# Regrouping the small matrix products of a delta-rule attention step that is woven into a feed-forward block

## The chip, the cores and the metric

The kernel runs on one core of one Trainium2 chip. The metric is the device time of one execution in microseconds (us), smaller is better. A core has five engines with a queue each: TensorE (PE in the profile; PEld are its weight loads), VectorE (DVE), ScalarE (ACT), GpSimd (POOL) and SyncE (SP, which issues transfers). They run side by side and wait for one another through semaphores; each takes its own instructions in the order of its queue. Products land in PSUM, which has eight banks of 512 fp32 columns on 128 partitions.

## The reference

A delta-rule attention over 4 x 8 heads of 768 tokens with 48 dimensions each, and after it a feed-forward block with a PReLU:

```python
# q, k, v: (4, 8, 768, 48); beta: (4, 8, 768)
k_n = k / (norm(k, axis=-1) + 1e-6)
state = zeros(B, H, D, D)
for t in range(S):
    y[:, :, t] = q[t] @ state
    v_old      = state.T @ k_n[t]
    state      = state + beta[t] * outer(k_n[t], v[t] - v_old)
x = y.transpose(0, 2, 1, 3).reshape(3072, 384)
h = x @ w_in                                      # (3072, 2048)
g = maximum(h, 0) + alpha * minimum(h, 0)
return g @ w_out                                  # (3072, 384)
```

All in fp32.

## The kernel before

The sequence is cut into 12 chunks of 64 tokens. A *step* n is one chunk of one pair of batches, 16 heads; there are 24 steps, and steps alternate between the two pairs, so step n continues the state of step n - 2. Inside a chunk the recurrence is a triangular system. Its 32 x 32 diagonal blocks are inverted on VectorE for four steps at once (`eliminate(m)`, where group m holds steps 4m to 4m + 3); the rest is small products on TensorE, 16 of them for each name below, in quarters of the array (64 x 64):

- `grams(n)`: k times k, the system's entries; made several steps ahead, as `eliminate` needs four steps of them
- `flips`: transposes of k and q through the identity, with copies by ScalarE
- `placing(n)`: ScalarE puts the inverted blocks where the products want them (`diag`, `inv`)
- `between_1(n)`, `between_2(n)`: the block of the inverse off the diagonal, in two products with a copy between them
- `through_state(n)`: what the old state gives to the values, the scores and the output (two products)
- `solve(n)`: the inverse times the right-hand side, giving `u`
- `outputs(n)`, `next_state(n)`: scores times `u` for the output, k times `u` for the state
- `to_ffn(n)`: transposes of the output for the feed-forward block

The feed-forward block of an earlier chunk is a generator of pieces: `ffn_in` (48 pieces a chunk, each a 128 x 128 by 256 product) and `ffn_out_fast` (28 pieces of two products of 192 columns; seven products of half matrices in place of eight). After each pair of `ffn_in` columns ScalarE and VectorE apply the PReLU. `weave` interleaves generators by shares. From step 4 on:

```python
def attention(n):
    place(n + 1, (0,))
    through_state(n)
    between_1(n + 1)
    yield
    solve(n)
    grams(n + EARLY)            # EARLY = 8
    between_2(n + 1)
    scale_v(n + 1)
    yield
    outputs(n)
    next_state(n)
    load_late(n + 2)
    squares(n + EARLY + 1)
    yield
    flips(n + EARLY + 1, n + 2)
    to_ffn(n)
    weigh(n + EARLY + 1)        # square root on ScalarE, reciprocal on VectorE
    load_early(...); load_q(n + 3); load_v(n + 3)
    yield

for n in range(NJ, N):          # NJ = 4, N = 24
    gens = [(attention(n), 4), (placing(n + 1, (1, 2, 3)), 24)]
    if n % NJ == 0 and n < N - NJ:
        m = n // NJ + 1
        blocks, left = eliminate(m), WHOLE + (PIECES if m > 2 else 0)   # 39, later 43 pieces
        share = -(-left // 3)
    if n % NJ < 3 and n < N - NJ:
        gens.append((part(blocks, share), share))
    if n < NJ + 2:
        gens.append((part(late, 12), 12))          # second product of chunk 1
    else:
        parts = IN_PARTS - 4 if n % 2 == 0 else FAST_PARTS + 4     # 44 or 32
        gens.append((part(tail, parts), parts))
    # ... weight_sums in steps 5 to 7
    weave(*gens)
```

One product with its reader, as each of them was written:

```python
def solve(n):
    p = ps_big()[:, :, 0 : G * D].rearrange("p a (g d) -> p a g d", a=2, g=G)   # own tile, two banks
    for g, a, t in quarters():                                                  # 16 products
        nc.tensor.matmul(p[half(t ^ a), a, g], inv[n % NE][half(t), a * G + g], rhs_[n][half(t), a, g])
    us[n] = work.tile([128, 2, G, D], FP32, name="u")
    nc.vector.tensor_tensor(out=us[n], in0=p, in1=..., op=ALU.mult)
```

`ps_big` hands out three tiles of two banks in turn; two single banks serve the feed-forward block.

Of the kernel before, what the change touches and what calls it, by code (L numbers as in the profile page):

```python
# [41 lines left out]
def kernel(  # L42
# [50 lines left out]
    NXT = 2  # L93

# [223 lines left out]
    def prep(n):  # L318

        if n >= N:  # L320
            return
        squares(n)
        weigh(n)
# [10 lines left out]
    def weigh(n):  # L334
        if n >= N:
            return
        c, bp = steps[n]
        norm = stats[n]
        nc.scalar.sqrt(norm, norm)
        nc.scalar.activation(norm, norm, ACT.Copy, bias=1e-6)  # L340
        rec = work.tile([128, H], FP32, name="rec")
        nc.vector.reciprocal(rec, norm)
        wgt = work.tile([128, 3, G], FP32, name="wgt", bufs=EARLY + 3)
        nc.gpsimd.tensor_tensor(out=beta_t[:, c, bp], in0=beta_t[:, c, bp], in1=rec, op=ALU.mult)
        nc.gpsimd.tensor_tensor(
            out=wgt[:, 0:2],
            in0=beta_t[:, c, bp].rearrange("p (g a) -> p a g", a=2),
            in1=rec.rearrange("p (g a) -> p a g", a=2),
            op=ALU.mult,
        )  # L350
        stats[n] = (norm, wgt)

    def flip(src, p):
        for g in range(G):
            nc.tensor.transpose(  # L355
                p[:, g * 128 : (g + 1) * 128],
                src[:, 2 * g : 2 * g + 2].rearrange("p h d -> p (h d)"),
                ident,
            )

    def flips(n_k, n_q):

        both = n_k < N and n_q < N
        p = ps_big() if both else None
        copies = []
        if n_k < N:
            p_k = p[:, 0] if both else ps_one()
            flip(early(n_k), p_k)
            k_t[n_k] = work.tile([128, G, 128], FP32, name="k_t", bufs=EARLY + 1)
            copies.append((k_t[n_k], p_k))  # L370
        if n_q < N:
            p_q = p[:, 1] if both else ps_one()
            flip(q_pad[n_q % NQ], p_q)
            q_t[n_q] = beside[steps[n_q][1]][:, :, :, D : D + C]
        for dst, src in copies:
            nc.scalar.copy(dst.rearrange("p g i -> p (g i)"), src)  # L376
        if n_q < N:
            nc.scalar.copy(  # L378
                q_t[n_q].rearrange("p t g i -> p g t i"),
                p_q.rearrange("p (g t i) -> p g t i", g=G, t=2),  # L380
            )
# [4 lines left out]
    def grams(n):  # L386

        if n >= N:
            return
        p = ps_big()[:, :, 0 : G * C].rearrange("p a (g i) -> p a g i", g=G)  # L390
        for g, a, t in quarters():
            nc.tensor.matmul(  # L392
                p[half(t), a, g], k_t[n][dims(a), g, half(t)], k_t[n][dims(a), g, half(t)]
            )
        w = stats[n][1][:, 0:2, :, None].to_broadcast([128, 2, G, HB])
        for dst, cols in (
            (gather(n), slice(0, HB)), (right[n % EARLY][:, 1:], slice(HB, C))
        ):
            nc.vector.tensor_tensor(  # L399
                out=dst.rearrange("p (a g) i -> p a g i", a=2), in0=p[:, :, :, cols], in1=w,  # L400
                op=ALU.mult,
            )
        keep(n)
# [231 lines left out]
    def between_1(n):  # L635

        if n >= N:
            return
        p = ps_big()[:, :, 0 : G * HB].rearrange("p a (g i) -> p a g i", a=2, g=G)
        for g, a, t in quarters():  # L640
            nc.tensor.matmul(  # L641
                p[half(t ^ a if changes(n) else t), a, g],
                right[n % EARLY][half(t), a * G + g : a * G + g + 2].rearrange("p b i -> p (b i)"),
                diag[n % NE][half(t), a * G + g, 0:HB],
            )
        nc.scalar.copy(
            mid[n % 2].rearrange("p (a g) i -> p a g i", a=2)[:, :, :, 0:HB], p
        )

    def between_2(n):  # L650
        if n >= N:
            return
        p = ps_big()[:, :, 0 : G * HB].rearrange("p a (g i) -> p a g i", a=2, g=G)
# [8 lines left out]
        nc.vector.tensor_tensor(out=to, in0=to if changes(n) else own, in1=p, op=ALU.add)  # L662
# [12 lines left out]
    def through_state(n):  # L675
        c, bp = steps[n]
        if c == 0:
            rhs_[n] = by_parity(nv[n])
            return
        p = ps_big()[:, :, 0 : G * (D + C)].rearrange("p a (g e) -> p a g e", g=G)  # L680
# [4 lines left out]
        p_y = ps_big()[:, :, 0 : G * D].rearrange("p a (g d) -> p a g d", g=G)  # L685
# [7 lines left out]
        for to, own, a in (  # L693
            (slice(0, 128), slice(0, 128), 0), (half(0), half(1), 1), (half(1), half(0), 1)
        ):
            nc.vector.tensor_tensor(  # L696
                out=r[to, a], in0=v_in[to, a], in1=p[own, a, :, 0:D], op=ALU.subtract
            )
        masked(n, p[:, :, :, D : D + C])
        y = work.tile([128, H, D], FP32, name="y")  # L700
        nc.scalar.copy(by_parity(y), p_y)  # L701
        rhs_[n], ys[n] = r, y

    def solve(n):
        p = ps_big()[:, :, 0 : G * D].rearrange("p a (g d) -> p a g d", a=2, g=G)
# [5 lines left out]
        nc.vector.tensor_tensor(  # L711
            out=us[n], in0=p,
            in1=stats[n][1][:, 0:3:2, :, None].to_broadcast([128, 2, G, D]), op=ALU.mult,
        )

    def outputs(n):
        c, bp = steps[n]
        p = ps_big()[:, :, 0 : G * D].rearrange("p a (g d) -> p a g d", a=2, g=G)
# [4 lines left out]
        if c == 0:  # L723
            ys[n] = work.tile([128, H, D], FP32, name="y")
            nc.scalar.copy(by_parity(ys[n]), p)
        else:
            nc.vector.tensor_tensor(
                out=by_parity(ys[n]), in0=by_parity(ys[n]), in1=p, op=ALU.add
            )

    def next_state(n):
        c, bp = steps[n]
        if c < NCH - 1:
            p = ps_big()[:, :, 0 : G * D].rearrange("p t (g d) -> p t g d", g=G)
# [5 lines left out]
            for a in range(2):  # L740
                x = state[bp][dims(a)]
                nc.vector.tensor_tensor(out=x, in0=x, in1=p[dims(a)], op=ALU.subtract)

# [219 lines left out]
    def weave(*gens):  # L963

        live = [[0.0, i, 1.0 / n, g] for i, (g, n) in enumerate(gens)]
# [9 lines left out]
    SHARES = 4  # L975

    def attention(n):


        place(n + 1, (0,))  # L980
        through_state(n)
        between_1(n + 1)
        yield
        solve(n)
        grams(n + EARLY)
        between_2(n + 1)
        scale_v(n + 1)
        yield
        outputs(n)
        next_state(n)  # L990
        load_late(n + 2)
        squares(n + EARLY + 1)
        yield
        flips(n + EARLY + 1, n + 2)
        to_ffn(n)
        weigh(n + EARLY + 1)
        load_early(n + EARLY + 1 + NKE)
        load_q(n + 3)
        load_v(n + 3)
        yield  # L1000
# [3 lines left out]
    def busy(n, p=None):  # L1004

        p = ps_one() if p is None else p
        while n > 0:
            x = p[:, 0 : int(512 * min(n, 1))]
            nc.tensor.matmul(  # L1009
                x, ident, k_t[NJ - 1].rearrange("p g i -> p (g i)")[:, 0 : x.shape[-1]]  # L1010
# [3 lines left out]
    def pair(n):  # L1014

        both = (n, n + 1)
        for i in both:
            through_state(i)
        yield
        for i in both:  # L1020
            solve(i)
            yield
        for i in both:
            outputs(i)
            next_state(i)
# [9 lines left out]
    def ready(n):  # L1035
# [7 lines left out]
        for i in both:  # L1043
            between_1(i)
# [5 lines left out]
        for i in both:  # L1050
            between_2(i)
# [23 lines left out]
    def first_chunk(mask, convert):  # L1075
# [20 lines left out]
        for i in both:  # L1096
            place(i, (1,), True)
            between_1(i)
        busy(0.5, ps_ffn())
        for i in both:  # L1100
            place(i, (2,))
            between_2(i)
        for i in both:
            through_state(i)
            solve(i)
        busy(0.5, ps_ffn())
        outputs(0)
        convert(4)
        next_state(0)
        outputs(1)  # L1110
        next_state(1)
# [9 lines left out]
    def statics(first, last):  # L1121
        if first > 0:
            squares(first)
        for n in range(first, last + 1):
            if n < last:
                squares(n + 1)
            weigh(n)
# [4 lines left out]
            if n > first:  # L1132
                grams(n - 1)
            yield
        grams(last)
# [102 lines left out]
    def prelude(n):  # L1238
        place(n)
        yield  # L1240
        between_1(n)
        yield
        between_2(n)
        yield
        scale_v(n)
        yield

    def catch_up():
        for n in range(FIRST + NJ, EARLY + NJ):
            grams(n)  # L1250
# [3 lines left out]
            weigh(n + 1)  # L1254
            load_early(n + 1 + NKE)
            yield

    late = ffn_out(1)
    few = OUT_PARTS // 4
    weave((prelude(NJ), 4), (catch_up(), 2 * (EARLY - FIRST)), (part(late, few), few))  # L1260
# [6 lines left out]
    tail = feed_forward()  # L1267
    for n in range(NJ, N):

        gens = [(attention(n), SHARES), (placing(n + 1, (1, 2, 3)), SHARES * PLACING)]  # L1270

        if n % NJ == 0 and n < N - NJ:
            m = n // NJ + 1
            blocks, left = eliminate(m), WHOLE + (PIECES if m > 2 else 0)
            share = -(-left // 3)
        if n % NJ < 3 and n < N - NJ:
            gens.append((part(blocks, share), share))
        if n < NJ + 2:
            gens.append((part(late, (OUT_PARTS - few) // 2), (OUT_PARTS - few) // 2))
        else:  # L1280
            parts = IN_PARTS - 4 if n % 2 == 0 else FAST_PARTS + 4
            gens.append((part(tail, parts), parts))
        if n == NJ + 1:
            gens.append((weight_sums(0, 0, 3), 3))
        elif n == NJ + 2:
            gens.append((chain(weight_sums(1, 0, 3), weight_sums(0, 3, 4)), 4))
        elif n == NJ + 3:
            gens.append((weight_sums(1, 3, 4), 1))
        weave(*gens)
# [32 lines left out]
```

## Time and profile before

| | |
|---|---|
| time, median of 3 (lowest to highest) | 685.09 us (684.9 to 686.08) |
| span of the profiled execution | 683.6 us |
| TensorE busy, products | 660.0 us, 9359 |
| VectorE busy, instructions | 471.3 us, 1162 |
| ScalarE busy, instructions | 249.4 us, 586 |
| HBM read and written | 31.56 and 4.72 MB |

How to read it: a product of fp32 operands appears as more than one record of TensorE (two for a large or small product, one for a transpose), and the records overlap, as products are pipelined. So the time a product costs is read from the distance between starts, not from the length of a record. `64*48 64x48` after a group's name is the part of the array (rows*columns) and the shape of the result. The number after "L" is the line of the kernel. "[1.70 <-DVE prod L477]" says that the engine stood idle for 1.70 us and what ended it. Lines to know: L840 is `ffn_in`, L904 `ffn_out_fast`, L882 the plain second product of the first chunks, L355 the flips, L751 `to_ffn`, L392 `grams`, L641 and L656 `between_1` and `between_2`, L682 and L687 `through_state`, L707 `solve`, L720 `outputs`, L736 `next_state`; on VectorE L477 and L483 are the elimination, L852 the PReLU, L711 the multiply that makes `u`.

### The profile page before, as it was taken

What the parts mean: (1) busy time and instruction counts of PE and PEld (TensorE: products, weight loads), DVE (VectorE), ACT (ScalarE), POOL (GpSimd) and SP (SyncE); (2) the same over time, 40 slices, a digit from 0 to 9 for tenths busy, and PEclk for the clock granted to TensorE, in tenths of its full rate; (3) what the DMA queues carried; (4) which work ended last, traced back from release to release, by engine and by line L of the source; (5) the groups of instructions that cost most, each with busy time, mean ns of one, the idle gap of its engine ahead of it and who ended that gap; (6) DMA issues with size and microseconds to landing.
All of it is one profiled execution on the core that took longest, in us unless ns stands there. A gap on an engine that the chain in (4) does not pass through costs nothing.

```text
span 683.6 us, 21618 instructions
## 1 busy us (share of the span) xinstructions
PE 660.0 (97%) x9359; PEld 570.2 (83%) x9359; DVE 471.3 (69%) x1162; ACT 249.4 (36%) x586; POOL 27.8 (4%) x95
## 2 busy tenths in 40 slices
PE   5989999999889999999999999999999999999997
PEld 4567777666678988988988988988989989989997
DVE  4966789879998379978479978379877255345261
ACT  4836756344434234235235235134034133231110
POOL 5000121000000000000000000000000000000000
PEclk9999999999999999999999999999999999999999
DMA  8847644211402112112112202201201211100000
GB/s 126 236 116 218 166 106 117 70 36 37 83 18 43 34 40 48 34 39 47 35 40 36 36 25 36 37 25 36 47 18 33 53 24 20 36 1 2 23 1 24
DMA packets 110958, 37.68 MB, mean 55 GB/s; under 512 B 104160, under 2 KB 107248, under 8 KB 110864
## 3 DMA queue, kind: packets, MB, share of 16 engines
q1 hardware_dynamic: 109088, 35.81, 24.0%
q8 instruction: 74, 1.21, 0.7%
q10 hardware_dynamic: 1776, 0.49, 0.4%
q14 instruction: 20, 0.16, 0.1%
HBM read 31.56 MB, written 4.72 MB: 53 GB/s over the span
## 4 chain that ended last, share of the span: by engine, by line
PE 79%; DVE 13%; ACT 3%; issue 1%; DMA 1%; SPq 1%; POOL 0%; ACTq 0%; DVEq 0%
PE p_ffn L840 32%; PE p_ffn L904 27%; PE p_big L355 3%; DVE block L483 2%; DVE prod L477 2%; PE p_big L682 2%; PE p_big L720 2%; PE p_big L707 2%; PE p_big L641 2%; PE p_big L1009 2%; DVE act L852 1%; PE p_big L656 1%; PE p_big L392 1%; PE p_big L687 1%; DMA ke<-in_k_dram 1%
## 5 line engine op out<-in xcount | busy, mean ns | idle before, releaser
L840 PE MATMUL p_ffn<-xt,w_in 128*128 128x256 f32 x1152 | 268.8, 385 | 6.2 <-DVE act L852 2.4
L840 PEld LDWEIGHTS p_ffn<-xt,w_in 128*128 128x128 f32 x1152 | 211.9, 190 | 37.0 <-issue 4.0
L852 DVE SCALAR_TENSOR_TENSOR act<-act,al_t,p_ffn 128x256 f32<-128x256 f32 x176 | 76.3, 475 | 56.8 <-ACT act L850 55.8
L850 ACT ACTIVATE act<-p_ffn 128x512 f32<-128x512 f32 x88 | 52.4, 596 | 129.7 <-PE p_ffn L840 120.1
L904 PE MATMUL p_ffn<-w_out,act 128*128 128x192 f32 x480 | 84.2, 329 | 0.3 <-DVE act L852 0.3
L904 PEld LDWEIGHTS p_ffn<-w_out,act 128*128 128x128 f32 x480 | 78.5, 190 | 1.9 <-DVE act L852 0.9
L483 DVE TENSOR_TENSOR block<-block,prod 128x30 f32<-128x30 f32 (+9 forms) x150 | 49.8, 332 | 5.2
L477 DVE TENSOR_TENSOR prod<-block 128x30 f32<-128x30 f32 (+9 forms) x150 | 48.9, 326 | 2.0
L924 DVE TENSOR_TENSOR o_sb<-u,p_ffn 128x192 f32<-128x192 f32 x40 | 13.2, 352 | 41.4 <-PE p_ffn L904 35.1
L378 ACT COPY beside<-p_big 128x512 f32<-128x512 f32 x24 | 14.0, 589 | 54.2 <-PE p_big L355 54.2
L376 ACT COPY k_t<-p_big 128x512 f32<-128x512 f32 x24 | 13.9, 580 | 51.6 <-PE p_big L355 51.5
L701 ACT COPY y<-p_big 128x384 f32<-128x384 f32 x22 | 10.5, 478 | 57.3 <-PE p_big L687 57.3
L904 PE MATMUL p_ffn<-space_out,sums 128*128 128x192 f32 x160 | 29.3, 326 | 0.0
L904 PE MATMUL p_ffn<-more,sums 128*128 128x192 f32 x160 | 29.3, 326 | 0.0
L696 DVE TENSOR_TENSOR r<-v_raw,p_big 64x192 f32<-64x192 f32 (+1 forms) x66 | 23.2, 352 | 7.3 <-PE p_big L682 6.2
L904 PE MATMUL p_ffn<-w_out,sums 128*128 128x192 f32 x160 | 27.7, 326 | 0.0
L904 PEld LDWEIGHTS p_ffn<-space_out,sums 128*128 128x128 f32 x160 | 26.6, 190 | 0.0
L904 PEld LDWEIGHTS p_ffn<-more,sums 128*128 128x128 f32 x160 | 26.6, 190 | 0.0
L441 ACT COPY same<-right 32x256 f32<-32x256 f32 x29 | 11.7, 402 | 40.1 <-DVE right L399 39.9
L904 PEld LDWEIGHTS p_ffn<-w_out,sums 128*128 128x128 f32 x160 | 25.8, 190 | 0.0
L924 DVE TENSOR_TENSOR u<-u,p_ffn 128x192 f32<-128x192 f32 x20 | 7.1, 354 | 26.4 <-PE p_ffn L904 26.3
L609 ACT ACTIVATE diag<-inverse,which 64x128 f32<-64x128 f32 (+2 forms) x60 | 24.2, 405 | 2.2 <-DVE inverse L453 1.3
(156 smaller groups left out, 948.5 us busy)
## 6 DMA issues: line engine op xcount, KB each, us to landing
w_out<-in_moe_w_in_dram SPq DMA_DIRECT2D x12, 512.0 KB, 5.0
qp<-in_q_dram SPq DMA_DIRECT2D x48, 96.0 KB, 2.9
v_raw<-in_v_dram SPq DMA_DIRECT2D x48, 96.0 KB, 2.9
kl<-in_k_dram SPq DMA_DIRECT2D x96, 48.0 KB, 2.4
out_dram<-o_sb SPq DMA_DIRECT2D x92, 48.0 KB, 1.6
space_out<-in_moe_w_out_dram SPq DMA_DIRECT2D x11, 384.0 KB, 4.3
ke<-in_k_dram SPq DMA_DIRECT2D x43, 96.0 KB, 3.1
w_out<-in_moe_w_out_dram SPq DMA_DIRECT2D x5, 384.0 KB, 3.6
```

Source lines behind the costliest of these rows:

```text
L355: nc.tensor.transpose(p[:, g * 128 : (g + 1) * 128], src[:, 2 * g : 2 * g + 2].rearrange("p h d -> p (h d)"), ident,)
L376: nc.scalar.copy(dst.rearrange("p g i -> p (g i)"), src)
L378: nc.scalar.copy(q_t[n_q].rearrange("p t g i -> p g t i"), p_q.rearrange("p (g t i) -> p g t i", g=G, t=2),)
L477: nc.vector.tensor_tensor(out=prod, in0=r[:, 0:j, j : j + 1].to_broadcast([128, j, n]), in1=r[:, j : j + 1, j + 1 : HB].to_broadcast([128, ...
L483: nc.vector.tensor_tensor(out=r[:, 0:j, j + 1 : HB], in0=r[:, 0:j, j + 1 : HB], in1=prod, op=ALU.add)
L609: nc.scalar.mul(out, x, which[rows, i : i + 1])
L696: nc.vector.tensor_tensor(out=r[to, a], in0=v_in[to, a], in1=p[own, a, :, 0:D], op=ALU.subtract)
L840: nc.tensor.matmul(p_h[:, i], w_in[:, t, (f + i) * 128 : (f + i + 1) * 128], xt[:, t], start=(t == 0), stop=(t == KT - 1),)
L850: nc.scalar.activation(g, p_h, ACT.Relu, scale=-1.0)
L852: nc.vector.scalar_tensor_tensor(out=g[:, i], in0=g[:, i], scalar=al_t[:, f + i : f + i + 1], in1=p_h[:, i], op0=ALU.mult, op1=ALU.add,)
L904: nc.tensor.matmul(p, x(i), w(i), start=(i == 0), stop=(i == FP - 1))
L924: nc.vector.tensor_tensor(out=to, in0=x, in1=p, op=ALU.add)
```

## The change

Each step has two bursts of small products instead of three. Burst A holds `outputs` and `next_state` of step n - 1 and `through_state` of step n; burst B holds `solve(n)`, `between_2(n + 1)`, `between_1(n + 2)` and `grams(n + 9)`. The products of a burst are issued back to back; products whose results fit together share one PSUM tile, and what reads them is issued after the burst (functions return the readers as a list, which `now` runs). `weigh` is split, so that the reciprocal comes later in VectorE's queue than the square root in ScalarE's. The Gram matrices are made one step earlier, the elimination of a group runs over four steps, and the feed-forward pieces come in fixed stretches between the bursts. The flips write and copy 112 rows of their result instead of 128 (two heads of 48, the second from row 64). Its purpose is to change less often between large and small products.

```diff
+    ROWS = C + D                                   # 112
 def flip(src, p):
         nc.tensor.transpose(
-            p[:, g * 128 : (g + 1) * 128],
-            src[:, 2 * g : 2 * g + 2].rearrange("p h d -> p (h d)"),
+            p[0:ROWS, g * 128 : (g + 1) * 128],
+            src[:, 2 * g : 2 * g + 2].rearrange("p h d -> p (h d)")[:, 0:ROWS],
             ident,
         )
 ...
-    def solve(n):
-        p = ps_big()[:, :, 0 : G * D].rearrange("p a (g d) -> p a g d", a=2, g=G)
+    def solve(n, p=None):
+        p = region(p, G * D, g=G)
 ...
-        nc.vector.tensor_tensor(
+        return [lambda: nc.vector.tensor_tensor(
             out=us[n], in0=p, ...
-        )
+        )]
 ...                                 # the same for the other products
-    def attention(n):               # (above)
+    def burst_a(n):
+        b = ps_big()
+        soon, later = [], []
+        if n > NJ:
+            soon += outputs(n - 1, b[:, :, 0:WY])
+            soon += next_state(n - 1, b[:, :, WY : 2 * WY])
+            later.append(lambda: load_late(n + 1))
+        if n < N:
+            p, y = ps_big(), ps_big()
+            soon += through_state(n, p[:, :, 0 : G * (D + C)], y[:, :, 0:WY])
+            if n + 1 == LATE:       # 8
+                soon += between_1(LATE, b[:, :, 2 * WY : 2 * WY + G * HB])
+            later.append(lambda: load_v(n + 3))
+        now(soon)
+        return later
+
+    def burst_b(n):
+        b, x = ps_big(), ps_big()[:, :, 0 : G * C]
+        soon = solve(n, b[:, :, 0:WY])
+        soon += between_2(n + 1, b[:, :, WY : WY + G * HB])
+        if n + 2 != LATE:
+            soon += between_1(n + 2, b[:, :, 2 * WY : 2 * WY + G * HB])
+        gram = grams(n + EARLY + 1, x)
+        now(soon + gram[:2])
+        return gram[2:] + [lambda: squares(n + EARLY + 2)]
+
+    def turn_round(n):
+        if n > NJ:
+            to_ffn(n - 1)
+        flips(n + EARLY + 1, n + 2)
+        later = weigh(n + EARLY + 1)
+        load_early(n + EARLY + 1 + NKE)
+        load_q(n + 3)
+        return later
 ...
 def prelude(n):                     # n = 4
     place(n)
+    place(n + 1, (0,))
     yield
     between_1(n)
+    between_1(n + 1)
     yield
     between_2(n)
-    yield
     scale_v(n)
     yield
+    place(n + 1, (1, 2, 3))
+    yield
 ...                                 # catch_up: one more grams and squares
+    def stretch(n, blocks, share, later, *gens):    # n feed-forward pieces, woven with
+        ...                                         # elimination (from 0.3 of it on) and `later` (from 0.5)
+    SHARES = {NJ + 2: (5, 6, 8), NJ + 3: (4, 4, 7)}                 # pieces of the elimination
+    TURNS = [(3, 3, 4), (3, 3, 4), (4, 4, 4), (3, 4, 4)]
+    FILL = {NJ: (4, 3, 3), NJ + 1: (3, 3, 2), NJ + 2: (2, 16, 12)}  # feed-forward pieces
+    FILLS = [(12, 16, 12), (12, 12, 12)]
 for n in range(NJ, N):
+    later = burst_a(n)
+    stretch(fill[0], blocks, share[0], later, *extra[0])
+    later = turn_round(n)
+    stretch(fill[1], blocks, share[1], later, *extra[1])
+    ...                             # every fourth step: place(n + 2, (0,)), next group
+    later = burst_b(n)
+    ...
+    stretch(fill[2], blocks, share[2], later + scales, *after, *extra[2])
+    ...                             # after step 6: group 2 must be done, group 3 begins
+stretch(12, iter(()), 0, burst_a(N))
+to_ffn(N - 1)
 for _ in tail:
     pass
```

## The prediction

> **What bounds the kernel now.** I read, in this order, the busy totals, the slices of the span, the chain of work that ended last, the TensorE timeline of one steady stretch, and the stretches by attention step. Totals, clock and chain:
>
> ```profile
> PE 660.0 (97%) x9359; PEld 570.2 (83%) x9359; DVE 471.3 (69%) x1162; ACT 249.4 (36%) x586; POOL 27.8 (4%) x95
> PEclk9999999999999999999999999999999999999999
> PE 79%; DVE 13%; ACT 3%; issue 1%; DMA 1%; SPq 1%; POOL 0%; ACTq 0%; DVEq 0%
> ```
>
> TensorE is the bound, at full clock, so a gain can only come from products that TensorE does faster or from waits it no longer has. The number of products isn't changed. So I look at what a change of product size costs. The timeline of TensorE in a steady step (columns: start us, length us, then the group):
>
> ```profile
> 396.96 5.02 PE L840 MATMUL p_ffn<-xt,w_in 128*128 128x256 f32 x22
> 401.90 0.68 PE L707 MATMUL p_big<-r,inv 64*64 64x48 f32 x32
> 402.40 0.66 PE L392 MATMUL p_big<-k_t 48*64 48x64 f32 x32
> 402.88 0.62 PE L656 MATMUL p_big<-diag,mid 64*64 64x32 f32 x32
> 403.43 5.45 PE L840 MATMUL p_ffn<-xt,w_in 128*128 128x256 f32 x24
> 408.81 0.68 PE L720 MATMUL p_big<-u,a_t 64*64 64x48 f32 x32
> 409.31 0.54 PE L736 MATMUL p_big<-u,kl 64*48 64x48 f32 x32
> 409.78 5.02 PE L840 MATMUL p_ffn<-xt,w_in 128*128 128x256 f32 x22
> 414.64 0.60 PE L355 MATMUL p_big<-ident,ke 128*128 128x128 f32 x4
> ...
> 640.79 20.88 PE L840 MATMUL p_ffn<-xt,w_in 128*128 128x256 f32 x96
> 661.51 5.36 PE L904 MATMUL p_ffn<-w_out,act 128*128 128x192 f32 x32
> ```
>
> The reader is to see the starts. Undisturbed, 96 records of the first feed-forward product take 661.51 - 640.79 = 20.72 us, 0.216 each. The 24 records between two bursts take 408.81 - 403.43 = 5.38, where 24 x 0.216 = 5.18 would do: 0.20 lost at the run's two ends. The burst of three small products takes 403.43 - 401.90 = 1.53 us. Single starts show groups of four records every 58 ns, eight groups a product, so 3 x 0.464 = 1.39: another 0.14 lost. Together **0.34 us a burst**. The burst of two gives the same: 0.97 us, against 0.464 + 8 x 0.045 = 0.82 (L736 steps at 45 ns), and the 0.20 beside it. Transposes (L355) follow the large products at full rate.
>
> Then the stretches by attention step, steps 4 to 8 (columns: window and length, then busy us of PE, PEld, DVE, ACT, POOL):
>
> ```profile
> 154.28:169.27 14.99, 14.09 (x293) 9.77 (x292) 14.08 (x40) 7.88 (x22) 0.45 (x3) 1.00 0.16 31
> 169.27:185.62 16.35, 14.37 (x292) 9.77 (x291) 15.59 (x38) 6.55 (x18) 0.51 (x2) 1.00 0.40 77
> 185.62:214.64 29.02, 26.08 (x357) 21.51 (x356) 25.83 (x63) 11.55 (x27) 1.57 (x4) 1.00 0.25 48
> 214.64:240.76 26.12, 26.12 (x392) 25.09 (x393) 14.11 (x31) 7.62 (x20) 0.41 (x2) 1.00 0.18 33
> 240.76:266.50 25.74, 25.74 (x384) 22.37 (x387) 21.30 (x55) 10.78 (x25) 0.41 (x2) 1.00 0.23 47
> ```
>
> From step 7 TensorE has no gap. In steps 4 to 6 (60.36 us) VectorE is busy 55.50 and TensorE stops now and then, for instance here:
>
> ```profile
> 199.26 2.40 PE L840 MATMUL p_ffn<-xt,w_in 128*128 128x256 f32 x10 [1.70 <-DVE prod L477]
> 206.41 1.97 PE L840 MATMUL p_ffn<-xt,w_in 128*128 128x256 f32 x8 [0.55 <-DVE act L852]
> ```
>
> There VectorE sets the pace, and a step's length is its queue of work.
>
> **What the Trainium skill says.** The page "TensorEngine Tiling (Array Packing)", section "Key Properties", says that changing the tiling mode, not just the tile, drains TensorE. The trace agrees: of the 0.34 us above, single starts put about a third on the way from 128*128 to 64*64 and the rest on the way back, while going from 64*64 to 48*64 (L707 to L392) costs nothing to speak of. The page "PSUM — Partial Sum Buffer", section "PSUM bank collisions raise a hardware error", wants readers and TensorE kept apart by bank, not address. In the new kernel several products of a burst share one pair of banks, so the first reader waits for the last writer of that tile; before, each product had its own tile, and no trace here shows the sharing yet. "Perfetto Trace Analysis", section "Optimization Strategy", says that a kernel can have regimes with different most-contended engines; steps 4 to 6 against the rest are such a case.
>
> **The change part by part.**
>
> 1. *Two bursts instead of three.* Before, a step has through_state + between_1, solve + grams + between_2, and outputs + next_state. After, outputs and next_state of step n-1 stand ahead of through_state of step n, and between_1 joins solve, between_2 and grams. The products are the same: 3 + 3 + 2 a step become 4 + 4. Steps 4 to 23 had 20 x 3 = 60 bursts; now there are 20 of each kind and one last for the outputs of step 23, 41. Of the 19 saved, 15 lie from step 8 on (48 become 33), where TensorE is the bound: 15 x 0.34 = **5.1 us saved**. The four of steps 4 to 7, 1.4 us, count only if TensorE sets the pace there.
>
> 2. *The flips write 112 rows instead of 128.* The transposes stream the same 128 columns of the identity; they start every 0.109 us now (L355: 0.43 for four) and will then. Copies have as many elements per partition. Zero.
>
> 3. *Dependencies.* State products of step n use the state of batch pair n mod 2, which the outputs burst before has updated; next_state(n-1) writes the other one. So nothing inside a burst waits for VectorE. From solve to outputs there are 12 feed-forward pieces, 12 x 0.432 = 5.2 us, for one VectorE multiply of 0.55 us (L711) behind the end of the burst. From through_state to solve there are 28 or 24. That is ample if VectorE's queue is short. Bursts now stand at multiples of six pieces, where one pair of feed-forward columns ends; the old cut left a wait of 0.17 us on the activation each second chunk of 51 us. Some new wait of that size may come where VectorE's queue is long after a burst: I put it at +0.5 us net.
>
> 4. *The elimination is spread over four steps instead of three.* In steps 8 and on this lowers the peaks of VectorE and is worth nothing, as TensorE doesn't wait there. In the early regime it costs: group 2 must still end with step 6, and 15 pieces of group 3 now come in step 7: four transposes of 0.61, a mask of 1.22 and ten pairs of 0.35 to 0.75, some 9.5 us. VectorE in steps 4 to 7 had 55.50 + 14.11 = 69.6 us; less feed-forward work there (16 pieces fewer) takes off some 1.4. So 69.6 + 9.5 - 1.4 = 77.7 us.
>
> 5. *Feed-forward pieces moved.* Steps 4 to 7 held 24 late output pieces and 44 + 32 = 76 of the tail; now 24 and 24 + 36 = 60. The 16 missing pieces are of the second product, 0.65 us each, 10.4 us that come later. Steps 4 to 7 took 240.76 - 154.28 = 86.5 us, so they break even at 76.1. VectorE's work is 77.7, but some 5 us of it stand in the queue behind what the burst of step 8 needs. So the burst can start at about 73, or 75 with 2 us of idle (before, VectorE idled 4.9 in steps 4 to 6). That is **0 to 3 us saved; I take 1**, in which the 1.4 of point 1 is included.
>
> 6. *The prelude* places the left part of step 5 earlier and does two between_1 in one burst; before, TensorE waited 0.9 us for a scaled copy of ScalarE ahead of the second. It also does one more Gram product, which a later step is spared. **0.5 saved.**
>
> Sum: -5.1 + 0.5 - 1 - 0.5 = -6.1. The median of 685.1 gives 679.0; I take 679.5, as point 5 rests on a queue with no gaps.
>
> **The rivals.** *Rival A: VectorE takes over.* In steps 4 to 7 its work is 77.7 us against 76.1 at break-even; with the old idle of 5 us the steps end some 6 us late and eat the gain: 684 to 686. For it: 55.50 busy of 60.36, and point 4. Against it: the pieces are woven in by shares, the square root is taken well ahead of its reciprocal, and idle of VectorE came mainly from such waits. *Rival B: new waits in each step.* If outputs wait for the solve's multiply behind other work, or the shared banks hold up a burst, at 0.3 us a step that is 6 us: again about 685. Against it: 5.2 us of slack and VectorE busy 70 to 90% of a step. *Rival C: the switch isn't the cost*, and a longer burst loses as much as two: then only points 5 and 6 remain, 683. Against it: 0.34 is the same for bursts of two products and of three.
>
> **Range and chances.** All rivals right together end near 688, all parts at their best (6.4 for the switches, 3 for early steps, 1 for the prelude) near 674.5. I put 80% on 675 to 684.5. Faster by over 2% needs 671.4, which no part offers: 0.03. Slower by over 2% needs 698.8, a new wait of a microsecond in each step: 0.02.
>
> **What would show it.** Right: TensorE's timeline has two bursts a step, a chunk of two steps shorter by 2 x 0.34 us (51.2 to 50.5 around 340 to 440 us), idle still near zero from step 8 on, and the burst of step 8 beginning at 226 to 231 us instead of 240.76, with 16 pieces more left to do. Wrong: TensorE idle in steady steps with VectorE named (u, act or y); the solve burst of four products taking clearly more than 4 x 0.464 + 0.14 = 2.0 us; VectorE busy through steps 4 to 7 with the burst of step 8 later than 232.

## The result, and the profile after

| | before | after |
|---|---|---|
| time, median of 4 (lowest to highest) | 685.59 us (684.9 to 687.79) | 691.84 us (689.12 to 692.29) |
| span of the profiled execution | 683.6 us | 690.4 us |
| start of `through_state` of step 4, then of step 8 | 154.28, 240.69 | 156.24, 239.89 |
| from `through_state` of step 8 to the end | 442.89 | 450.49 |

The kernel became slower: ratio 1.0084, interval 1.0057 to 1.011. The predicted 679.5 us and its range missed it; even the sign was wrong. Totals, clock and chain of the profile after:

```profile
PE 660.5 (96%) x9359; PEld 573.0 (83%) x9359; DVE 467.9 (68%) x1162; ACT 250.1 (36%) x585; POOL 28.2 (4%) x95
PEclk9999999999999999999999999999999999999999
PE 77%; DVE 13%; ACT 5%; SPq 2%; issue 2%; DMA 1%; POOL 0%; ACTq 0%
```

On this page the two kernels look alike, which is the first lesson: a change of 6.8 us in 690 has to be looked for in stretches between the same events. Lines have moved: L872 is `ffn_in`, L936 and L914 the second products, L360 the flips, L783 `to_ffn`, L407 `grams`, L660 and L674 `between_1` and `between_2`, L704 and L709 `through_state`, L734 `solve`, L747 `outputs`, L763 `next_state`; on VectorE L884 is the PReLU, L489 the mask of the elimination, L753 the addition that makes `y`.

The timeline of TensorE in a steady step after the change:

```profile
411.70 0.68 PE L734 MATMUL p_big<-r,inv 64*64 64x48 f32 x32
412.20 0.63 PE L674 MATMUL p_big<-diag,mid 64*64 64x32 f32 x32
412.85 0.67 PE L660 MATMUL p_big<-diag,right 64*64 64x32 f32 x32
413.33 0.67 PE L407 MATMUL p_big<-k_t 48*64 48x64 f32 x32
413.94 5.45 PE L872 MATMUL p_ffn<-xt,w_in 128*128 128x256 f32 x24
419.32 0.68 PE L747 MATMUL p_big<-u,a_t 64*64 64x48 f32 x32
...
420.96 0.63 PE L709 MATMUL p_big<-beside 48*64 48x48 f32 x32
421.52 1.78 PE L872 MATMUL p_ffn<-xt,w_in 128*128 128x256 f32 x7
```

There are two bursts a step, of 413.94 - 411.70 = 2.24 and 421.52 - 419.32 = 2.20 us, and the 24 records between them take 5.38 us as before. Most bursts B take 2.02 us, as the prediction has it; in this one `between_1` starts 0.2 us late, as ScalarE's `diag` ends at 412.80. The steady part did get shorter. From step 12 to step 16 four steps took 102.37 us before and take 101.41 now, which holds 0.44 us of new waiting, but one Gram product (0.46) less.

Now the stretches of steps 4 to 7, each from one `through_state` to the next (columns: window and length, busy us of PE, PEld, DVE, ACT and POOL, then the granted clock of TensorE, DMA share and GB/s):

```profile
156.24:168.22 11.98, 11.98 (x285) 8.59 (x288) 8.83 (x28) 6.48 (x19) 0.82 (x4) 1.00 0.33 61
168.22:185.75 17.53, 13.04 (x299) 9.29 (x292) 15.05 (x37) 6.87 (x19) 0.62 (x2) 0.90 0.32 59
185.75:210.52 24.77, 21.52 (x314) 17.11 (x306) 21.80 (x57) 10.07 (x24) 0.41 (x2) 0.93 0.21 42
210.52:239.89 29.37, 26.64 (x413) 23.66 (x405) 28.24 (x67) 12.82 (x33) 0.91 (x2) 0.94 0.16 29
```

The reader is to see two things. Neither TensorE nor VectorE is busy throughout: of 83.65 us TensorE is idle for 10.5 and VectorE for 9.7 (before, 5.8 and 16.8 of 86.41). And TensorE's clock is no longer 1.00 here; before, it was in all these steps.

The sum, with the 16 feed-forward pieces (10.4 us) that were moved behind step 8 set against both of the last two terms: step 4 begins 1.96 later; steps 4 to 7 take 83.65 + 10.4 - 86.41 = 7.64 longer; from step 8 on it is 450.49 - 10.4 - 442.89 = 2.80 shorter. Together +6.8, the difference of the spans. Some products moved too: one Gram product and one `between_1` (0.93 us) from behind step 8 into the prelude, and the `to_ffn` of step 7 (0.33) to behind step 8. So 0.93 of the first term is moved work, and of the last term only 2.2 are gained.

Two lines of the list of waits point at the cause (what waits, for what: us in total, times, longest):

```profile
ACT mid L666 <- DVE inv L680: 40.6, 17, 6.5
DVE norm L332 <- ACT ksq L330: 16.6, 10, 3.4
```

The first wait is new; 13.0 of its 40.6 us lie in steps 4 to 7. The second grew: in steps 4 to 7 it is 4.7 us, and before the change VectorE had none of it there. `mid` and `inv` read different products of burst B, which now lie in one shared PSUM tile, and ScalarE's copy starts only when VectorE has read its part. The timeline of step 5 shows what follows:

```profile
167.33 0.37 ACT L666 COPY mid<-p_big 128x256 f32<-128x256 f32 x1 [4.54 <-DVE inv L680]
171.38 0.51 ACT L330 ACTIVATE ksq<-ke 128x384 f32<-128x384 f32 x1
171.92 0.55 DVE L332 TENSOR_REDUCE norm<-ksq 128x8 f32<-128x384 f32 x1 [1.94 <-ACT ksq L330]
173.53 0.55 DVE L753 TENSOR_TENSOR y<-y,p_big 128x384 f32<-128x384 f32 x1
174.23 0.52 PE L783 MATMUL p_big<-ident,y 128*128 128x128 f32 x3 [2.46 <-DVE y L753]
175.16 1.10 PE L360 MATMUL p_big<-ident,ke 128*112 128x128 f32 x4 [0.42 <-DVE beside L771]
```

ScalarE stands for 4.54 us, then works through the scaled copies of the placing, so the squares come late; VectorE stands for 1.94 us on them; the addition behind them is late, and TensorE waits 2.46 us for `y`. The last line shows a second cost: four transposes take 1.10 us instead of the 0.60 they take at full clock. From 175.06 to 178.47 us the clock records say half speed, and again for 3.413 us from 192.13 and from 222.85, each after a wait of 2.15 us or more.

### The profile page after: what moved, and what is told of

Read it like the earlier page. It is cut to its first block, busy times and chain, and to the rows that moved or that the text cites. A ratio compares the mean times of both kernels' runs of the same rounds, so it can differ in the third digit from the quotient of the medians.

```text
span 690.4 us, 21593 instructions
## 1 busy us (share of the span) xinstructions
PE 660.5 (96%) x9359; PEld 573.0 (83%) x9359; DVE 467.9 (68%) x1162; ACT 250.1 (36%) x585; POOL 28.2 (4%) x95
## 4 chain that ended last, share of the span: by engine, by line
PE 77%; DVE 13%; ACT 5%; SPq 2%; issue 2%; DMA 1%; POOL 0%; ACTq 0%
PE p_ffn L872 32%; PE p_ffn L936 27%; PE p_big L360 2%; PE p_big L734 2%; PE p_big L704 2%; PE p_big L660 2%; PE p_big L1062 2%; SPq L120 2%; PE p_big L747 2%; DVE prod L496 1%; PE p_big L674 1%; DVE block L502 1%; DVE act L884 1%; DVE block L472 1%; ACT diag L628 1%
## 5 line engine op out<-in xcount | busy, mean ns | idle before, releaser
L872 PE MATMUL p_ffn<-xt,w_in 128*128 128x256 f32 x1152 | 267.1, 385 | 7.7 <-ACT k_t L381 2.2
L872 PEld LDWEIGHTS p_ffn<-xt,w_in 128*128 128x128 f32 x1152 | 214.5, 191 | 39.3 <-ACT k_t L381 3.6
L884 DVE SCALAR_TENSOR_TENSOR act<-act,al_t,p_ffn 128x256 f32<-128x256 f32 x176 | 76.3, 475 | 76.7 <-ACT act L882 76.5
L936 PE MATMUL p_ffn<-w_out,act 128*128 128x192 f32 x480 | 82.2, 328 | 0.0
L936 PEld LDWEIGHTS p_ffn<-w_out,act 128*128 128x128 f32 x480 | 77.6, 190 | 0.5
L785 ACT COPY xt<-p_big 128x384 f32<-128x384 f32 x22 | 10.5, 476 | 82.0 <-PE p_big L783 81.9
L936 PE MATMUL p_ffn<-space_out,sums 128*128 128x192 f32 x160 | 29.3, 326 | 0.0
L936 PE MATMUL p_ffn<-more,sums 128*128 128x192 f32 x160 | 29.3, 326 | 0.0
L727 ACT COPY y<-p_big 128x384 f32<-128x384 f32 x22 | 10.5, 477 | 48.3 <-PE p_big L709 48.3
L936 PE MATMUL p_ffn<-w_out,sums 128*128 128x192 f32 x160 | 27.6, 326 | 0.0
L936 PEld LDWEIGHTS p_ffn<-space_out,sums 128*128 128x128 f32 x160 | 26.6, 190 | 0.0
L936 PEld LDWEIGHTS p_ffn<-more,sums 128*128 128x128 f32 x160 | 26.6, 190 | 0.0
L936 PEld LDWEIGHTS p_ffn<-w_out,sums 128*128 128x128 f32 x160 | 26.3, 190 | 0.0
L666 ACT COPY mid<-p_big 128x256 f32<-128x256 f32 x24 | 8.8, 371 | 48.0 <-DVE inv L680 40.6
L771 DVE TENSOR_TENSOR beside<-beside,p_big 48x384 f32<-48x384 f32 x44 | 24.1, 548 | 0.3
L332 DVE TENSOR_REDUCE norm<-ksq 128x8 f32<-128x384 f32 x24 | 13.0, 547 | 16.6 <-ACT ksq L330 16.6
```

The lines of the kernel that those rows point to most:

```text
L872: nc.tensor.matmul(p_h[:, i], w_in[:, t, (f + i) * 128 : (f + i + 1) * 128], xt[:, t], start=(t == 0), stop=(t == KT - 1),)
L884: nc.vector.scalar_tensor_tensor(out=g[:, i], in0=g[:, i], scalar=al_t[:, f + i : f + i + 1], in1=p_h[:, i], op0=ALU.mult, op1=ALU.add,)
L936: nc.tensor.matmul(p, x(i), w(i), start=(i == 0), stop=(i == FP - 1))
```

## The experiments

Every one is a change to the new kernel. One kernel's times spread by several us, and its longer executions report a lower mean clock (the kernel before: 684.02 us at 0.999, 693.35 at 0.983). Six of the ten traces after the change have spells of half clock in the first 100 us; that such spells make the spread is likely, but one trace a kernel can't show it. So where a few us matter I compare stretches between the same bursts. Break-even with the kernel before is 86.41 - 10.4 = 76.0 us for steps 4 to 7, and for the rest 442.89 + 10.4 = 453.3; the moved products of 0.33 and 0.93 us are not taken off.

| kernel | median us | ratio to before (interval) | start of step 4 | step 4 to step 8 | step 8 to end |
|---|---|---|---|---|---|
| after | 691.84 | 1.0084 (1.0057 to 1.011) | 156.24 | 83.65 | 450.49 |
| own tile | 688.86 | 1.0042 (1.0006 to 1.0077) | 155.65 | 78.40 | 450.41 |
| filler | 692.83 | 1.0112 (1.0089 to 1.0134) | 156.47 | 81.30 | 450.47 |
| split | 700.0 | 1.0216 (1.0199 to 1.0233) | 160.82 | 83.78 | 454.08 |
| late only | 687.48 | 1.0027 (1.0004 to 1.0051) | 158.82 | 76.93 | 453.22 |
| prelude | 690.27 | 1.0053 (1.003 to 1.0076) | 162.48 | 79.62 | 450.39 |
| order | 685.76 | 0.999 (0.997 to 1.001) | 156.88 | 77.16 | 449.37 |
| rows | 692.83 | 1.0094 (1.0061 to 1.0127) | 156.56 | 83.41 | 450.48 |
| filler before `u` | 693.02 | 1.0084 (1.0062 to 1.0107) | 159.80 | 81.15 | 450.40 |
| best of both | 684.41 | 0.9984 (0.9961 to 1.0008) | 155.34 | 76.96 | 449.95 |

### A tile of its own for between_1

```diff
-            soon += between_1(n + 2, b[:, :, 2 * WY : 2 * WY + G * HB])
+            soon += between_1(n + 2)
```

> The changed kernel with one difference: in burst B, between_1(n + 2) gets a PSUM tile of its own again, so ScalarE's copy of it need not wait until VectorE has read solve and between_2 from the same two banks. Theory 1a (the shared tile puts ScalarE behind VectorE in steps 4 to 6, and then VectorE behind ScalarE): the waits of ScalarE's copy for VectorE's inv (40.6 us in 17 waits) are gone, VectorE's idle on the norm in steps 4 to 6 (1.9 and 0.7 us) goes, burst A of step 8 starts 2 to 4 us before 239.9, time 687.5 to 690. Theory 1b (what counts in these steps is TensorE's waits and its halved clock after them): 691 to 692. Rival B (the shared tiles cost in every step): also the steady steps get shorter, under 687.

Measured: 5.25 us off steps 4 to 7, more than I expected; from step 8 on 450.41, as before the edit, so the sharing costs nothing there. In step 5 the same instructions now stand like this:

```profile
168.68 0.51 ACT L330 ACTIVATE ksq<-ke 128x384 f32<-128x384 f32 x1
169.28 0.55 DVE L332 TENSOR_REDUCE norm<-ksq 128x8 f32<-128x384 f32 x1
170.88 0.55 DVE L753 TENSOR_TENSOR y<-y,p_big 128x384 f32<-128x384 f32 x1
```

Counted from the start of step 5 (168.22 and here 167.64), the squares are 2.1 us earlier, VectorE doesn't wait for them, and `y` is 2.1 earlier. By steps:

| us | step 4 | step 5 | step 6 | step 7 | half clock in steps 5 to 7, us |
|---|---|---|---|---|---|
| before | 14.98 | 16.36 | 29.01 | 26.06 | none |
| after | 11.99 | 17.53 | 24.77 | 29.37 | 3.4 in each of 5, 6, 7 |
| own tile | 11.99 | 15.53 | 22.81 | 28.06 | 6.8, at the start of 6 |
| filler | 11.99 | 18.17 | 23.07 | 28.08 | 3.4, around the start of 6 |
| prelude | 11.99 | 15.42 | 22.90 | 29.32 | 6.8 in 6, 3.4 in 7 |
| order | 11.99 | 15.49 | 22.31 | 27.36 | none |

Steps 5 and 6 gain 2.00 and 1.96, where the shared tile had made the waits: 3.96 us, the largest single cause. Step 7 gains 1.31, and this isn't the tile, as that burst's `between_1` still lies in the shared one. TensorE waits there as it did, only no half clock follows; after the change, and then with the tile of its own:

```profile
221.97 6.24 PE L872 MATMUL p_ffn<-xt,w_in 128*128 128x256 f32 x20 [2.15 <-ACT k_t L381]
217.41 2.83 PE L872 MATMUL p_ffn<-xt,w_in 128*128 128x256 f32 x12 [2.14 <-DVE act L884]
```

Seven traces bear this out. With a spell step 7 takes 29.37 us (after), 29.34 (split), 29.35 (rows) and 29.32 (prelude), without one 28.06 (own tile), 28.08 (filler) and 28.01 (filler before `u`): a spell there costs 1.3 us.

### Products of no use while TensorE waits

Three products of 512 columns, whose result nobody reads, stand ahead of `to_ffn` in steps 5 and 6, and behind the flips in step 7. They keep TensorE active and add 9 x 0.86 = 7.7 us of work beside the waits.

```diff
+    def filler(p):
+        for _ in range(3):
+            nc.tensor.matmul(p, ident, w_in[:, 0, 0:512])
 ...                                 # called in turn_round(n) for n = 5, 6 and 7
```

> The changed kernel with filler products added where TensorE waited long in steps 5, 6 and 7 (three products of 512 columns, 2.6 us, whose results nobody reads; the outputs are untouched). Theory 1b (the halved clock after each long wait costs the early steps): the granted clock stays at 1.0, burst A of step 8 starts about 3 us before 239.9 (one spell of 1.7 us right on the path, another shared with VectorE), time 688.5 to 689.5. Theory 1a (VectorE's queue sets these steps and the clock is a bystander): 691 to 692.5.

Measured: of the three half-clock spells one is left (185.06 to 188.47 us), and steps 4 to 7 take 81.30 us, 2.35 less, with 7.7 us more work. The transposes of step 5:

```profile
171.84 2.74 PE L1042 MATMUL p_ffn<-w_in,ident 128*128 128x512 f32 x6
175.38 0.65 PE L360 MATMUL p_big<-ident,ke 128*112 128x128 f32 x4 [0.42 <-DVE beside L771]
```

They take 0.65 us where they took 1.10. So the spells come from the waits; the one that is left begins at the end of a wait of 3.21 us for `u`, which grew from 1.62. What they cost by themselves shows in step 7 alone (28.08 instead of 29.37): in step 6 waits are shortened too, and in step 5 the filler is longer than the wait. The median, 692.83, is a miss and doesn't show the gain, probably because of early spells (the other three executions have mean clocks of 0.985 to 0.990, the profiled one 0.996); the profiled executions differ by 690.4 - 688.2 us.

### The saved switch put back

From step 9 on, four or six feed-forward pieces stand between `next_state` and `through_state`, which makes three bursts a step again and leaves all else.

```diff
+        if LATE < n < N:
+            now(soon)
+            soon = []
+            for _ in range(6 if n % 2 else 4):
+                next(tail)
 ...                                 # as many fewer in the stretch behind burst A
```

> The changed kernel, but from step 9 on six or four feed-forward pieces stand between outputs + next_state and through_state, so that burst A is two bursts again (15 more changes of product size; same products, same pieces). Theory 1 (a burst costs 0.34 us whatever its length): 15 x 0.34 = 5.1 us slower than the changed kernel, about 697. Rival C (a longer burst loses as much as two): the same as the changed kernel, 691 to 693.

Measured: from step 8 on 454.08, 3.6 more, although the listed waits of TensorE there (those over 0.15 us) fell from 1.87 to 0.65 us. So 15 switches cost 3.6 + 1.2 = 4.8 us, 0.32 each. The timeline shows one:

```profile
425.75 0.54 PE L763 MATMUL p_big<-u,kl 64*48 64x48 f32 x32
426.21 2.86 PE L872 MATMUL p_ffn<-xt,w_in 128*128 128x256 f32 x12
429.00 1.00 PE L704 MATMUL p_big<-beside,k_t 48*64 48x112 f32 x32
```

`next_state` holds TensorE for 0.46 us instead of 0.36, and 12 records for 2.79 instead of 12 x 0.216 = 2.59: 0.30 in all. Rival C, the switch isn't the cost, is refuted. (The median of this kernel also carries, probably, a start of step 4 that is 4.6 us late in its profiled execution, from early half-clock spells; it isn't the split.)

### Two bursts from step 8 on alone

The prelude and steps 4 to 7 are as before the change, with 16 pieces taken out of step 7; the Gram product and the `between_1` that burst B wants ahead (0.93 us) stand at the end of step 7.

```diff
-        if n > NJ:                      # in burst_a and turn_round
+        if n > LATE:
+    for n in range(NJ, LATE):           # the old attention, three bursts
+        gens = [(attention(n), 4), (placing(n + 1, (1, 2, 3)), 4 * PLACING)]
 ...                                    # the old prelude and weaving; shares of elimination for steps 8 to 10
```

> Steps 4 to 7 and what is ahead of them scheduled as in the kernel before (three bursts, elimination in three steps), with 16 feed-forward pieces fewer in step 7; from step 8 on two bursts as in the changed kernel. Theory 1 (the two bursts save 0.34 us each and the early steps spent it): 685.1 less 5.1 for 15 bursts, plus 2 for new small waits, 681 to 683.5. Rival B (the regrouped steady steps give the loss): 688 or more.

Measured: a miss. Steps 4 to 7 are at break-even (76.93 with the 0.93 us), but 453.22 us from step 8 on gives back all that the switches save: the elimination's shares that I chose for steps 8 to 10 made TensorE wait 0.45 and 1.85 us for the PReLU in step 9, beside the waits that the new kernel has. The run does isolate the prelude. From the burst at 78 to 83 us to the start of step 4 it takes 75.98 us, against 76.01 in the kernel before and 78.09 in the new one.

### Placing after the prelude's Gram work

With the tile of its own, and the placing of step 5 moved behind the prelude, which was to end VectorE's first wait for the squares.

```diff
-        place(n + 1, (1, 2, 3))
-        yield
+    place(NJ + 1, (1, 2, 3))            # after the prelude
 ...                                    # between_1(n + 2) in a tile of its own
```

> As the own-tile run (between_1 of burst B in a PSUM tile of its own), and ScalarE places the blocks of step 5 after the prelude's last Gram work instead of ahead of it. There VectorE waited 2.08 us for ScalarE's square of k just before step 4's subtraction. Theory 1a (VectorE's queue, held up by ScalarE, sets steps 4 to 7): that wait goes and burst A of step 4 to burst A of step 8 takes 76.5 us instead of 78.4; time 2 us under the own-tile run. If TensorE's waits set it: still 78.

Measured: a miss, 79.62 against 78.40 without it. VectorE's wait fell from 2.08 to 1.48 us only, and step 4 took 11.99 us with and without the edit: TensorE sets its length, so that wait cost nothing. The 1.2 us are the half-clock spell in step 7.

### No elimination between burst A and the turn

With the tile of its own. In every fourth step (7, 11, 15, 19) the elimination's pieces move out of the first stretch into the other two.

```diff
-    SHARES = {NJ + 2: (5, 6, 8), NJ + 3: (4, 4, 7)}
-    TURNS = [(3, 3, 4), (3, 3, 4), (4, 4, 4), (3, 4, 4)]
+    SHARES = {NJ + 2: (5, 6, 8), NJ + 3: (0, 6, 9)}
+    TURNS = [(3, 3, 4), (3, 3, 4), (4, 4, 4), (0, 5, 6)]
```

> As the own-tile run, and no elimination pieces in the first stretch (between burst A and the transposes) of steps 7, 11, 15 and 19; they come in the other two stretches. Theory 1c (TensorE waits there for a PReLU on VectorE that stands behind the readers of burst A and a mask of 1.22 us): the waits of 2.2 us in step 7, 1.1 us at 319 and 0.66 us at 422 shrink by a microsecond or go; from step 8 to the end 448.8 us instead of 450.4, step 7 shorter by 1; time 2 to 3 us under the own-tile run. If the wait is TensorE's own (readers of the shared tile): no change.

The reason for it, in the timeline of step 11 after the change:

```profile
324.17 1.22 DVE L489 TENSOR_TENSOR block<-block,inside 128x1024 f32<-128x1024 f32 x1
325.82 0.47 DVE L884 SCALAR_TENSOR_TENSOR act<-act,al_t,p_ffn 128x256 f32<-128x256 f32 x1
326.44 3.91 PE L872 MATMUL p_ffn<-xt,w_in 128*128 128x256 f32 x17 [1.05 <-DVE prod L496]
```

The timeline names `prod`, but TensorE goes on when the two PReLU instructions, which free its PSUM bank, have ended; they stood behind the mask of 1.22 us, and that behind burst A's readers. Measured: 1.24 us off steps 4 to 7 and 1.04 off the rest, 2.3 in all, as expected; the waits of steps 11 and 15 are gone. Of the 1.24, 0.70 are in step 7, where the order was changed (its wait fell from 2.14 to 1.60 us), and 0.50 in step 6, ahead of the edit. The clock is full throughout here: the same wait of 2.82 us for `u`, which half clock followed in "own tile", brought none. So 6.8 us of half clock in step 6 cost only 0.5: TensorE, at full clock, then waits 1.87 us for `y`.

### 128 rows in the flips

```diff
-    ROWS = C + D
+    ROWS = 128
```

> The changed kernel with the flips writing and copying 128 rows again instead of 112 (also the filler products of the start contract over 128 rows again). Prediction's step 2 (no effect): 691.8, within 1 us, transposes 0.109 us apart, bursts at the same places.

Measured: 83.41 and 450.48, the stretches of the new kernel. The rows are worth nothing either way. The run also serves as a second trace of the new kernel: steps 4 to 7 take 11.98, 17.49, 24.59 and 29.35 us, with three spells of half clock at nearly the same places.

### Filler ahead of the wait for u

With the tile of its own, three products of no use ahead of burst A in step 6.

```diff
+        if n == NJ + 2:
+            for _ in range(3):
+                nc.tensor.matmul(ffn_banks[turn[0] ^ 1], ident, w_in[:, 0, 0:512])
```

> As the own-tile run, with three filler products of 512 columns (2.6 us, read by nobody) ahead of burst A of step 6, where TensorE waited 2.87 us for u and then ran 6.8 us at half clock. Theory 1b (the halved clock delays what VectorE waits for): no spell of half clock there, burst A of step 4 to burst A of step 8 shorter by 1.5 to 3 us than 78.4. If VectorE's queue alone sets these steps: 78 again.

Measured: a miss, 81.15 against 78.40. The wait for `u` fell from 2.82 to 0.25 us, but the next one, for `y`, is 2.90, and half clock came there, from 192.33 to 199.15 us. Filling one of two waits moved the spell, 6.8 us as before, and the filler's 2.6 us came on top.

### The parts that paid, together

Two bursts from step 8 on, the old steps 4 to 7 and prelude, the tile of its own, and no elimination in the first stretch of every fourth step.

```diff
+            soon += between_1(n + 2)
+    TURNS = [(3, 3, 4), (3, 3, 4), (4, 4, 4), (0, 5, 6)]
+    SHARES = {LATE: (6, 7, 6), LATE + 1: (2, 3, 6), LATE + 2: (4, 5, 4)}
 ...                                 # the rest as in "late only"
```

> Steps 4 to 7 as in the kernel before (as in the late-only run), two bursts from step 8 on with between_1 in its own tile, no elimination pieces in the first stretch of steps 11, 15 and 19, and in steps 8 to 10 fewer pieces where TensorE waited in the late-only run (0.5 and 2.0 us in step 9). Theory 1 (early steps and queue order spent the gain of the bursts): burst A of step 4 to burst A of step 8 76 to 77 us, from there to the end 449.0 instead of 453.2, time 681 to 682.5 where the clock is granted in full, ratio 0.994 to 0.997. If the gain of the bursts is lost to something else: 685 or more.

Measured: 684.41 us, ratio 0.9984 with an interval that holds 1. In steps 4 to 7 76.96; from step 8 on 449.95, 3.4 below break-even, with one wait of 1.4 us left in step 9. It is clearly better than the new kernel and, over all executions, not distinguishable from the kernel before. But where the mean clock was 0.999 or more, it took 681.6 to 683.18 us in five executions, and the kernel before, measured beside it, 683.91 to 685.78 in eleven (medians 682.19 and 685.03). So two bursts from step 8 on, with these mends, are worth 2.8 us, as was expected for a full clock. The executions with less clock hide it; whether the edits make these more frequent is not known.

## Why the prediction was wrong

The sum was -6.1 and the spans differ by +6.8. Of these 12.9 us, 8.6 lie in steps 4 to 7 (-1 predicted, +7.6 measured), 2.5 in what stands ahead of step 4 (-0.5, +1.96) and 1.8 from step 8 on (-4.6, -2.8).

**Step 1, the switches: right.** Predicted 0.34 us each, 5.1 in all. Putting them back costs 0.30 (timeline) to 0.32 (stretch) each. In the kernel "order" the steps from 8 on are 3.9 below break-even, 3.3 without the products that only moved, with 0.6 us more of listed waits than before and another 0.65, too short to be listed, inside three bursts B (2.25 and 2.24 us instead of 2.02, 1.94 instead of 1.53): about 4.6 for 15, 0.30 each.

**Step 2, the flips: right**, zero.

**Step 3, new waits: too small.** I put them at 0.5 net. Listed waits of TensorE from step 8 on went from 0.3 to 1.9 us. The four-product bursts hand VectorE more readers at once, and PReLU queues behind them; two of the three waits, 1.66 us, went when the order of the elimination was changed. So the queue's order made these, not the dependencies, which had slack as predicted.

**Steps 4 and 5, the early steps: the failed step.** "So the burst can start at about 73, or 75 with 2 us of idle." The work was well counted: VectorE is busy for 73.9 us of the stretch. The idle wasn't: 9.7 us instead of 2. That is 83.65 instead of 75, and the predicted gain of 1 became a loss of 7.6. I worked out the length from one engine's work and took its queue to have no gaps, though the change itself put a new chain from VectorE to ScalarE and back into it. Even with the tile of its own VectorE is busy for 72.7 us of 78.40, idle for 5.7: the 2 us were too few there as well. The runs split the loss: 4.0 us in steps 5 and 6 by the shared tile (with the half clock that its waits brought), 1.3 by the spell in step 7, 0.5 by the one in step 6 that came and went without an edit, 0.7 by the elimination ahead of the PReLU in step 7, and 1.15 left over break-even (1.5 with the `to_ffn` that fell behind step 8); what made this rest isn't settled.

**Step 6, the prelude: wrong sign.** Predicted -0.5; from the burst at 78 us on it takes 78.09 instead of 76.01, +2.1. The wait of 0.9 us that I meant to save is gone, but it stood in step 4 (at 156.63 us), and in the prelude listed waits went from 4.1 to 4.4. And the extra Gram product and the second `between_1` are 32 records more each, 16 groups of 58 ns, 0.93 us, and TensorE is busy for most of this stretch (71.8 of 76.0 us before). I had said that the extra product spares a later step, and had not charged it here. The other 0.9 of the 2.1 us isn't settled.

**The rivals.** Rival A had the right place and too little: it charged the old idle of 5 us, and the new chain brought 9.7. Rival B had the right cause in the wrong place: the shared banks do hold up a burst's readers, but in the early steps, not 0.3 us in each. I hadn't joined the two: a shared tile in the regime where VectorE's queue sets the length. Rival C is refuted.

With the causes found taken out, in "order", steps 4 to 7 lose 1.15 us, the prelude some 2.1, and from step 8 on 3.9 are gained, 0.93 us of products having moved from there into the prelude: near a draw, which is what was measured. That the 16 missing pieces cost something in steps 4 to 7 isn't shown: "late only" has them missing too, under three bursts, and is at break-even.

## What to carry to other kernels

When products are joined in one PSUM tile, their readers on different engines may no longer run side by side: ask for each reader which engine it now waits for, and what stands behind it in its own queue. Work out a stretch's length from the chain through its engines, not from the sum of one engine's work, above all where a change adds a link between two engines. Look at the waits before saving switches: here a wait of 2.15 us in step 7, where half clock followed it, cost another 1.3 us, as much as four switches.

## What the runs showed of the hardware

TensorE's clock went to half after waits of only 2.15 to 2.7 us (step 7 and steps 5 and 6 after the change), for 3.413 us each time, in other runs twice that; the starts 175.06, 192.13 and 222.85 are 5 and 9 times 3.413 us apart. The Trainium skill, page "TensorE: Matmul & The Clock Gate", section "What's actually happening", has a free-running window of 3413 ns, which agrees, and the throttled state after at least one idle window of about 3.4 us, which doesn't: no wait of TensorE in these steps was that long. Nor does the length alone decide: 2.14 us in step 7 brought no spell with the tile of its own, and 2.82 us in step 6 brought one in "own tile" and none in "order". Where the wait falls does. In every trace all spells start whole multiples of 3.413 us apart, so a spell, or the one at the program's end, gives the grid of windows. In the eleven traces 1711 windows at full clock lie between 100 and 640 us. The 14 in which TensorE was idle for 2.05 to 3.15 us were followed by half clock; the others, idle for 1.87 us at most, were not. The 2.14 us in "own tile" are split by the end of a window at 217.13 us into 1.87 and 0.28, the 2.82 us in "order" by one at 181.83 into 1.13 and 1.69. So whether a wait of 2 to 3 us brought half clock was partly luck, and so is the spell's share of what a run gained or lost. In the first 100 us idle time isn't all: spells start there behind windows with as little as 0.10 us of it, and no run shows why.
